# Making u and v as pairs by three products of w_in in place of four, in a fused FNet-mixing and spatial-gating kernel

## The chip, the cores and the metric

The kernel runs on one core of a Trainium2 chip. The metric is the device time of one execution in microseconds (us). Engines are called as the profile calls them: PE multiplies matrices, PEld loads its weights, DVE is the vector engine, ACT the activation engine, POOL the third elementwise engine, SP the engine that here only issues transfers.

## The reference

```python
X = fft(fft(x, axis=1), axis=2).real              # x: 8 x 3072 x 256
h = maximum(X @ w_in, 0)                          # w_in: 256 x 1024
u, v = h[..., :512], h[..., 512:]
v_n = (v - mean(v)) / sqrt(var(v) + 1e-6)         # over the last axis
v_s = einsum('ts,bsd->btd', w_spatial, v_n) + b_spatial[None, :, None]
out = (u * v_s) @ w_out                           # out: 8 x 3072 x 256
```

The largest part by far is the product with `w_spatial` (W below), 3072 x 3072, for each of the 8 batches.

## The kernel before

The transform over time is a sum of a part that is even in the time s and one that is odd. So with E the even part's product with `w_in` and O the odd part's, time s has E + O and time 3072 - s has E - O. The kernel keeps both parts in a tile `eo`, and the weights in `weo`. For time s it multiplies with `weo`, for time S - s with the same first half and the negated second, `wom`: two products for each, four for the two. In batch 0 it also turns W by transposes on PE, piece by piece, and writes it back to memory in the turned form; later batches only load it.

One batch is 24 steps: six chunks of 512 times, each with four groups g of six tiles of v. While PE makes the spatial products of batch b, the preparation of batch b + 1 (folds of x on DVE, the transforms, v) is put into the same steps. The parts that matter here, with cuts:

```python
psM = tile_pool(name="psM", bufs=4, space=PSUM)     # four banks, shared by all but pw
NWR = 6                                             # buffers for loaded pieces of W

def v_tile(b, i, eo, v, pr):                        # one tile of 128 times
    pv = psM.tile([P, DH], FP32, name="pv", tag="psM")
    for kt in range(2):                             # w: weo, or weo and wom for i >= 12
        nc.tensor.matmul(pv, lhsT=l, rhs=w, start=(kt == 0), stop=(kt == 1))
    nc.scalar.activation(out=r, in_=pv, func=AF.Relu)
    nc.vector.bn_stats(out=stt[:, jj, :], in_=r)
    nc.vector.bn_aggr(out=mv[:, jj, :], in_=stt[:, jj, :])
def v_root(pr): ...                                 # ACT: sqrt(var + eps) of two tiles
def v_norm(b, v, pr): ...                           # ACT scales one tile, DVE the other

def s_v(i):                                         # the queue's order, batches 1 to 7
    if i % 2 == 0 and i: v_norm(b, v, pr)           # of the two tiles before
    v_tile(b, i, eo, v, pr)

for dt in range(NDT):                               # one step
    spatial(cur["v"], wts[ti], pws[dt], g, dt)      # six matmuls of 512 columns
    if g == NG - 1: gts.append(gate(c, pws[dt], uts[dt]))
    piece()                                         # batch 0: turn one more piece of W
    ...                                             # project, u_tile, the step's preparation
```

## Time and profile before

1469.43 us is the median of four runs (1468.79 to 1474.39). The profiled execution spans 1471.1 us.

| | before |
|---|---|
| busy share PE / DVE / ACT / POOL | 93% / 50% / 32% / 9% |
| granted clock over the whole kernel | 0.975 |
| start to the first output tile's copy out of PSUM | 153.1 us |
| from there to the same copy of batch 1 | 191.4 us |
| the same from batch to batch, 1 to 6 (mean of 5) | 168.2 us |
| batch 6 to 7; batch 7 to the end | 163.5; 122.0 us |

The copy of a batch's first output tile (`ot`, on ACT, in its fifth step) I call the mark of a batch.

### The profile page before, as it was taken

The numbers are of one execution on the slowest core, as the hardware profiler recorded it, in microseconds if no ns is written. First come the engines' busy times: TensorE is split into PE (matmuls) and PEld (weight loads), VectorE is DVE, ScalarE is ACT, GpSimd is POOL, SyncE is SP. The second block draws the span as 40 slices with busy tenths as digits, with TensorE's granted clock in tenths as the row PEclk, the third lists the DMA queues.
The fourth block names the chain that finished last, engine by engine and source line by source line (L and its number), as shares of the span: only waits on it lengthen the run. The fifth ranks groups of instructions, "written<-read, shape, count | busy, mean of one in ns | idle before, by whom it ended". The sixth has DMA issues, their size and how long they took to land.

```text
span 1471.1 us, 18005 instructions
## 1 busy us (share of the span) xinstructions
PE 1372.1 (93%) x7071; PEld 673.5 (46%) x7071; DVE 740.0 (50%) x1491; ACT 464.2 (32%) x779; POOL 133.7 (9%) x187
## 2 busy tenths in 40 slices
PE   0667999999999999999999999999999999999998
PEld 0333455544444444444444444444444444444444
DVE  6757745555355634655344733565345643561212
ACT  3554235521244123431244113431244212441111
POOL 7622434410000000000000000000000000000000
PEclk9878999999999999999999999999999999999999
DMA  7863999795333543346334463336344443434441
GB/s 258 282 223 125 329 337 297 259 330 180 129 129 126 196 163 124 122 141 224 122 129 133 151 203 129 129 122 228 130 138 141 151 159 122 144 127 157 143 158 50
DMA packets 100597, 255.28 MB, mean 174 GB/s; under 512 B 13568, under 2 KB 60192, under 8 KB 100384
## 3 DMA queue, kind: packets, MB, share of 16 engines
q1 hardware_dynamic: 61440, 196.66, 39.4%
q10 hardware_dynamic: 29568, 44.05, 8.2%
q0 software_dynamic: 9504, 13.42, 2.8%
q8 instruction: 55, 0.90, 0.2%
q14 instruction: 30, 0.25, 0.0%
HBM read 210.80 MB, written 56.62 MB: 182 GB/s over the span
## 4 chain that ended last, share of the span: by engine, by line
PE 84%; DVE 7%; ACT 1%; issue 1%; ACTq 0%; DVEq 0%
PE pw L496 63%; PE po L512 6%; PE pu L488 5%; PE pv L454 5%; DVE tm L501 2%; PE pt L151 1%; PE pe L408 1%; DVE gt L504 1%; DVE sm L308 1%; DVE xt L328 1%; DVE stt L458 1%; DVE of L330 0%; DVE ef L312 0%; ACT v_t L472 0%; ACT r L457 0%
## 5 line engine op out<-in xcount | busy, mean ns | idle before, releaser
L496 PE MATMUL pw<-wt,v_t 128*128 128x512 bf16 x4608 | 1084.5, 382 | 37.6 <-DVE tm L501 23.4
L496 PEld LDWEIGHTS <-v_t 128*128 128x128 bf16 x4608 | 451.6, 98 | 581.2 <-issue 41.3
L501 DVE TENSOR_TENSOR tm<-pw,bbc 128x512 f32<-128x512 f32 x192 | 131.0, 682 | 263.5 <-PE pw L496 263.5
L490 ACT ACTIVATE ut<-pu 128x512 bf16<-128x512 f32 x192 | 114.6, 597 | 318.0 <-PE pu L488 213.2
L458 DVE BATCH_NORM_STATS2 stt<-r 128x6 f32<-128x512 f32 x192 | 132.6, 690 | 162.0 <-ACT r L457 162.0
L516 ACT COPY ot<-po 128x512 f32<-128x512 f32 x96 | 56.3, 586 | 309.6 <-PE po L512 308.0
L504 DVE TENSOR_TENSOR gt<-tm,ut 128x512 bf16<-128x512 f32 x192 | 135.8, 707 | 13.8 <-DVE tm L501 0.5
L457 ACT ACTIVATE r<-pv 128x512 f32<-128x512 f32 x192 | 111.0, 587 | 100.5 <-PE pv L454 91.3
L472 ACT ACTIVATE v_t<-r,rs 128x512 bf16<-128x512 f32 x96 | 78.1, 813 | 105.1 <-DVE rs L470 104.4
L512 PE MATMUL po<-wob,gt 128*128 128x256 bf16 x768 | 103.6, 279 | 1.4 <-DVE gt L504 1.4
L488 PE MATMUL pu<-eo_t,weo 128*128 128x512 bf16 x288 | 95.1, 385 | 2.4 <-ACT r L457 2.4
L454 PE MATMUL pv<-weo,eo_t 128*128 128x512 bf16 x288 | 94.7, 385 | 0.8 <-DVE wt L154 0.3
L512 PEld LDWEIGHTS <-gt 128*128 128x128 bf16 x768 | 76.8, 101 | 32.4 <-issue 3.3
L156 ACT COPY wt<-pt 128x768 bf16<-128x768 bf16 x53 | 42.0, 800 | 61.4 <-PE pt L151 61.0
L469 DVE RECIPROCAL rs<-rs 128x2 f32<-128x2 f32 x96 | 15.5, 162 | 89.0 <-ACT rs L465 89.0
L151 PE MATMUL pt<-ident,wb 128*128 128x128 bf16 x576 | 50.6, 231 | 6.9 <-ACT r L457 2.8
L454 PEld LDWEIGHTS <-eo_t 128*128 128x128 bf16 x384 | 37.2, 100 | 41.8 <-issue 2.7
L151 PEld LDWEIGHTS <-wb 128*128 128x128 bf16 x576 | 42.4, 104 | 29.0 <-issue 7.0
L474 DVE TENSOR_SCALAR v_t<-r,mv,rs 128x512 bf16<-128x512 f32 x96 | 52.7, 549 | 0.0
L146 POOL CAST wb<-wr 128x768 bf16<-128x768 f32 x48 | 42.6, 895 | 78.4 <-PE pt L151 46.9
L143 POOL CAST wb<-wr 128x768 bf16<-128x768 f32 x48 | 42.1, 887 | 70.3 <-PE pt L151 40.2
L410 ACT ACTIVATE eo_t<-pe,spb 128x384 bf16<-128x384 f32 (+1 forms) x32 | 35.8, 1117 | 37.8 <-PE pe L408 37.8
(218 smaller groups left out, 664.2 us busy)
## 6 DMA issues: line engine op xcount, KB each, us to landing
wt<-wtd SPq DMA_DIRECT2D x168, 768.0 KB, 4.4
wr<-in_moe_w_spatial_dram SPq DMA_DIRECT2D x96, 384.0 KB, 5.2
out_dram<-ot ACTq DMA_DIRECT2D x96, 256.0 KB, 3.9
wtd<-wt ACTq DMA_DIRECT2D x24, 768.0 KB, 5.3
xr<-in_x_dram POOLq DMA_DIRECT2D x32, 384.0 KB, 11.7
xt<-in_x_dram SPq DMA_DIRECT2D x21, 512.0 KB, 4.0
xt<-xr SPq DMA_DIRECT2D x21, 512.0 KB, 5.0
x<-in_x_dram SPq DMA_DIRECT2D x1, 1536.0 KB, 6.6
```

What stands on the lines that cost most here:

```text
L151: nc.tensor.transpose(pt[:, kk, :], wb[:, 128 * kk:128 * kk + 128], ident)
L454: nc.tensor.matmul(pv, lhsT=l, rhs=w, start=(kt == 0), stop=(kt == 1))
L457: nc.scalar.activation(out=r, in_=pv, func=AF.Relu)
L458: nc.vector.bn_stats(out=stt[:, jj, :], in_=r)
L472: nc.scalar.activation(out=v[:, i - 1, :], in_=r2[0], func=AF.Identity, scale=rs[:, 0:1], bias=rs[:, 2:3])
L488: nc.tensor.matmul(pu, lhsT=w, rhs=r, start=(kt == 0), stop=(kt == 1))
L490: nc.scalar.activation(out=ut, in_=pu, func=AF.Relu)
L496: nc.tensor.matmul(pw, lhsT=v[:, k, 128 * dt:128 * dt + 128], rhs=wt[:, kk, :], start=(k == 0), stop=(k == KT - 1))
L501: nc.vector.tensor_tensor(out=tm, in0=pw, in1=bbc[:, TC * c:TC * c + TC], op=ALU.add)
L504: nc.vector.tensor_tensor(out=gt, in0=tm, in1=ut, op=ALU.mult)
L512: nc.tensor.matmul(po[:, i, :], lhsT=gts[dt][:, t0:t0 + 128], rhs=wob[:, dt, :], start=(dt == 0), stop=(dt == NDT - 1))
L516: nc.scalar.copy(out=ot, in_=po)
```

## The change

Its intent: PE is full, so take products off it. With P = eo times weo (two products: E + O) and M = 2 O (one product with doubled weights, `wo2`), time s is P, and time S - s is P - M. ACT copies M out of PSUM, and DVE subtracts it from P. u is paired in the same way, so its chunks are reordered (`ORDER`) and the upper ones shifted by one row, which makes the last tile of chunk 3 of 127 rows plus the single row of time S/2. The W pieces pair columns likewise, the first nine are cast by ACT rather than POOL, and the folds of x move to steps without gates.

```diff
-NWR = 6
+NWR = 5
+ORDER = [0, 3, 1, 4, 2, 5]
+def t_base(c):
+    return TC * c if c < 3 else 2561 - TC * (c - 3)
...
+    def w_rows(c, r):
+        t0 = t_base(c) + P * r
+        if c == 3 and r == 3:
+            return [(0, P - 1, t0), (P - 1, 1, S // 2)]
+        return [(0, P, t0)]
...
-            nc.gpsimd.tensor_copy(out=wb, in_=wr)
+            if first:
+                nc.scalar.copy(out=o_, in_=i_)
+            else:
+                nc.gpsimd.tensor_copy(out=o_, in_=i_)
...
+    def v_pair(i, eo, pr):
+        for kt in range(2):
+            nc.tensor.matmul(pv, lhsT=eo[:, kt, sl], rhs=weo[:, kt, DH:], start=(kt == 0), stop=(kt == 1))
+        nc.tensor.matmul(pd, lhsT=eo[:, 1, sl], rhs=wo2[:, DH:], start=True, stop=True)
+        nc.scalar.activation(out=r[0], in_=pv, func=AF.Relu)
+    def v_minus(i, eo, pr, pv, pd):
+        nc.scalar.copy(out=m_, in_=pd)
+        nc.vector.tensor_tensor(out=r[1], in0=pv, in1=m_, op=ALU.subtract)
+        nc.vector.bn_stats(out=stt[:, 0, :], in_=r[0])
+        nc.scalar.activation(out=r[1], in_=r[1], func=AF.Relu)
...
+            if c == 3 and h == 1:       # output: 128 rows, 127 rows, one row
+                nc.scalar.dma_start(out=..., in_=ot[:, 0, :])
+                nc.scalar.dma_start(out=..., in_=ot[0:P - 1, 1, :])
+                nc.scalar.dma_start(out=..., in_=ot[P - 1:P, 1, :])
...
+                    if i:                                   # the queue's order of a pair
+                        st_[s][q].append(lambda i=i: self.vn(i - 1))   # scaling of i - 1
+                    st_[s][q].append(lambda i=i: self.va(i))           # products, first relu
+                    st_[s][q].append(lambda i=i: self.vb(i))           # copy, subtraction, statistics
+                    st_[s][q + 1].append(lambda i=i: self.vr(i))       # root
```

## The prediction

> **What bounds the kernel now.** I read, in order, the busy times of the page, busy time by stretch, the timelines of PE and VectorE (DVE) around one batch start, then the groups of instructions that the change touches.
>
> ```profile
> PE 1372.1 (93%) x7071; PEld 673.5 (46%) x7071; DVE 740.0 (50%) x1491; ACT 464.2 (32%) x779; POOL 133.7 (9%) x187
> ...
> 0.00:81.00 81.00, 27.18 (x170) 14.28 (x171) 57.49 (x89) 35.39 (x48) 53.08 (x90) 0.89 0.82 280
> 81.00:132.00 51.00, 37.25 (x189) 17.70 (x186) 28.11 (x74) 27.09 (x49) 9.78 (x12) 0.80 0.49 172
> 132.00:309.00 177.00, 170.21 (x1120) 93.42 (x1121) 108.15 (x203) 72.16 (x115) 70.83 (x85) 0.98 0.83 293
> 646.00:814.00 168.00, 164.81 (x812) 79.40 (x810) 85.04 (x179) 50.98 (x88) 0.00 (x0) 0.99 0.45 151
> 1319.00:1471.00 152.00, 146.65 (x734) 71.46 (x731) 35.72 (x58) 23.49 (x40) 0.00 (x0) 1.00 0.38 128
> ```
>
> The columns of a stretch are its length, then PE, weight load, DVE, ACT and POOL busy, the granted clock, the DMA share and GB/s. There are three stages. Up to 132 us (tables, folds, first tiles of v) PE has many gaps. From 132 to 309 us batch 0 also turns W, and DMA is 83% busy. Then come batches of 168 us, in which PE lacks only 3.2 us; the last one, with nothing to prepare, takes 152. So PE bounds batches 1 to 7. Its gap, at a batch's fourth step:
>
> ```profile
> 832.65 5.34 PE L496 MATMUL pw<-wt,v_t 128*128 128x512 bf16 x24
> 837.83 0.59 PE L488 MATMUL pu<-eo_t,weo 128*128 128x512 bf16 x2
> 838.26 4.21 PE L496 MATMUL pw<-wt,v_t 128*128 128x512 bf16 x18
> 845.66 2.72 PE L496 MATMUL pw<-wt,v_t 128*128 128x512 bf16 x6 [3.19 <-DVE tm L501]
> ...
> 844.85 0.17 DVE L341 COPY ho<-od 128x2 bf16<-128x2 bf16 x1
> 844.92 0.69 DVE L501 TENSOR_TENSOR tm<-pw,bbc 128x512 f32<-128x512 f32 x1
> ```
>
> The folds of x stand on DVE between the last gates of a chunk; the fourth gate is late, its PSUM bank is not free, and PE waits 3.19 us. The next six matmuls take 2.72 us, while twelve elsewhere in the chain take 2.59: 0.216 us each, or about double after the gap. The gap thus costs 3.2 + 1.4 + some 0.3 in the projection behind it = 4.9 us.
>
> The groups that I use:
>
> ```profile
> L501 DVE TENSOR_TENSOR tm<-pw,bbc 128x512 f32<-128x512 f32 x192 | 131.0, 682 | 263.5 <-PE pw L496 263.5
> L490 ACT ACTIVATE ut<-pu 128x512 bf16<-128x512 f32 x192 | 114.6, 597 | 318.0 <-PE pu L488 213.2
> L458 DVE BATCH_NORM_STATS2 stt<-r 128x6 f32<-128x512 f32 x192 | 132.6, 690 | 162.0 <-ACT r L457 162.0
> L457 ACT ACTIVATE r<-pv 128x512 f32<-128x512 f32 x192 | 111.0, 587 | 100.5 <-PE pv L454 91.3
> ...
> 77.84 0.29 ACT L465 ACTIVATE rs<-mv,epst 128x2 f32<-128x2 f32 x1 [1.75 <-DVE mv L459]
> 78.68 0.81 ACT L472 ACTIVATE v_t<-r,rs 128x512 bf16<-128x512 f32 x1 [0.54 <-DVE rs L470]
> 79.40 0.58 ACT L457 ACTIVATE r<-pv 128x512 f32<-128x512 f32 x1
> ```
>
> The last three give hand-over times: from a square root's start to the scaling of v is 0.84 us, and a following activation starts 0.72 us after that one.
>
> **What the Trainium skill says.** "TensorE: Matmul & The Clock Gate", section "Wait — 56ns, not 53.3ns?", gives 215.7 ns per warm matmul of 512 columns and 426.7 cold: the trace agrees (216, and about 450 after the gap). Its section "Architectural detail" calls the ACT and DVE queues strictly first in, first out: everything below rests on that, and the trace agrees (the late gate behind the folds). "ScalarE: Activation LUTs", section "What ACT_TABLE_LOAD costs", gives 186 ns + 0.833 ns per element, 613 ns for 512; the trace has 587 from PSUM. I take 0.61 us for the new relu from SBUF. "DMA: Bandwidth & Descriptors", section "Why a DMA increments its semaphore by 16 and not by 1", says that a transfer whose outer dimension is 127 runs on one of the 16 engines; the kernel before has no such transfer, so its trace shows nothing of it.
>
> **The change part by part.**
>
> 1. Fewer products. v needs 3 x 12 matmuls of 512 columns per batch in place of 48, u likewise: 24 fewer x 0.216 = 5.2 us per batch, 41.5 us in all, on the bounding engine. Added: the column of time S/2, two matmuls of 512 for v (0.43) and eight of one column for u (about 0.45, an estimate from the 0.055 us pitch of 128-column transposes). Net per batch 4.3.
>
> 2. Folds moved off the gate steps (now steps 0, 1, 4, 5, 8, 9 of a batch): the 4.9 us gap goes in batches 1 to 6, and about 4 us in batch 0.
>
> 3. What is added off PE. Each pair has one more ACT copy out of PSUM (0.59) and one DVE subtraction (0.69, as tm); v's second relu now starts only after the subtraction. In sum DVE gets 24 x 0.69 = 17 us per batch on 85, ACT nothing much for u and 12 x 0.6 for v on 51. Neither engine becomes full.
>
> 4. The serial chain of a v pair. In the new queue order ACT runs scaling of pair i-1, relu, copy, second relu, root of pair i, and only then scaling of i; each step waits for DVE. One turn: 0.72 (scaling to next start) + 0.49 (relu to next start) + 0.59 (copy) + 0.04 + 0.69 (subtract) + 0.04 + 0.61 (relu) + 0.04 + 0.69 (statistics) + 0.04 + 0.18 (aggregate) + 0.04 + 0.84 (root to scaling) = 5.0 us. Nothing of pair i overlaps pair i-1.
> The 12 pairs stand in steps 14 to 23 of a batch. PE's own time there: 40 groups of six spatial matmuls x 1.30 = 52, pairs 12 x 0.65 = 7.8, four u pairs 2.6, four projections 3.5: 66 us. The chain: 12 x 5.0 = 60; in each of the three gate steps (15, 19, 23) gate 0 (1.4) stands before one pair's reciprocal and gates 1 to 3 (4.2) before the next, less 0.4 of overlap: 5.2 x 3 = 15.6; the u pairs' copies and subtractions add about 1 us x 4. Sum about 80, which is 14 more than PE has.
> Can PE run ahead? A pair takes two of the four shared PSUM banks, so it can by about one and a half pairs. I walked the built queues bank by bank with these durations: PE waits about 5 us in steps 16 and 17 (a u product needs the bank that pair 3's copy frees), 5 in steps 20 and 21 (late gates, then pair 8's bank), 2 at the next batch's start (gates behind pair 11). I take 12.2 us per preparation.
>
> 5. Start. ACT casts nine W pieces (two casts of 384 elements, about 1.0 us, on top of a 0.8 us copy), so POOL, which in the kernel before casts while a 1.23 us fold takes 4.95, leaves DVE alone. DVE gains about 12 us up to the end of the folds, but ACT's nine pieces at about 2.5 us each, with the width products, end no earlier. I count zero. The nine pairs in batch 0's first three steps take 9 x 5.4 + 4 = 53 us, as the 51 now.
>
> 6. W in batch 0. The last rows of chunk 3 are loaded as 127 + 1, four times. If 127 rows use one engine: 390 KB at 348 GB/s / 0.96 / 16 = 22.6 GB/s (window 150 to 200 us) is 17 us each, against 5.2 now. They are wanted one step (17 to 20 us) apart, so most hides; I count 10 us.
>
> Sum. Batches 1 to 6: 168.0 - 4.9 - 4.3 + 12.2 = 171.0, +3 x 6 = +18. Batch 7: -2 (u only). Batch 0: -4.3 - 4 + 12.2 + 2 (W evacuations in the chain) + 10 = +16. Total +32: 1502 us.
>
> **Rivals.** (a) The chain hides behind PE. For it: no engine is full, and the present order, with pairs of tiles in twelve steps, never stalls there. Against: the 5.0 us turn and four banks. It would give 1502 - 7 x 12.2 = 1417, with the start in its favour 1405. (b) Batch 0 is bounded by DMA: 83% busy now, pieces of 1.5 KB rows in place of 3, and one engine holding a piece; wasted time could be 40 us, 1530. (c) The start gains the 12 us on DVE: 1490. (d) POOL casts slow the chain's DVE steps in batch 0 as they slow the folds: another 10 us.
>
> **Range and chances.** The chain's surplus is the difference of two sums near 70, so 7 us either way per batch is fair: 7 x 7 = 49 us at the extremes. With batch 0 at plus or minus 15, eight in ten lie in 1448 to 1540. Faster by 2% (under 1440) needs most stalls absent: 0.14. Within 2% (to 1499): 0.38. Slower: 0.48.
>
> **What would show it.** Right: a period near 171 us of which PE is busy 159; PE idle before pud, po and pd products, released by ACT copies and DVE subtractions, in steps 16, 17, 20 and 21; root-to-root time of v pairs 5 us or more; no 3.2 us gap in step 4; W pieces with landing times near 17 us. Wrong: a period near 159 us, with PE full during the pairs (rival a); or PE idle before transposes in 132 to 309 us (rival b).

## More of the kernel before

From the page, the shares of the chain that ended last; and from the groups, the scaling of v on ACT (busy us, mean ns, then idle time before it and what ended it):

```profile
PE 84%; DVE 7%; ACT 1%; issue 1%; ACTq 0%; DVEq 0%
...
L472 ACT ACTIVATE v_t<-r,rs 128x512 bf16<-128x512 f32 x96 | 78.1, 813 | 105.1 <-DVE rs L470 104.4
```

PE carries 84% of the chain. ACT waits 104 us before its scalings, but beside a full PE, so they cost nothing.

## The result

The changed kernel takes 1555.62 us, the median of four runs (1552.24 to 1559.46): slower by a ratio of 1.058 (95% interval 1.0546 to 1.0613). A ratio here is the mean time of one kernel's fast runs over the mean of the other's of the same rounds, so not quite the ratio of the medians quoted. The profiled execution spans 1553.5 us at a granted clock of 0.959. The direction is as predicted; 1555.62 lies outside the range of 1448 to 1540.

The page of the changed kernel: busy times, the shares of the chain that ended last, and two groups.

```profile
PE 1365.8 (88%) x6955; PEld 657.5 (42%) x6955; DVE 854.3 (55%) x1715; ACT 516.7 (33%) x897; POOL 153.0 (10%) x278
...
PE 57%; DVE 18%; ACT 9%; DMA 5%; issue 4%; POOL 3%; ACTq 2%; SPq 1%; DVEq 0%; POOLq 0%
...
L505 ACT ACTIVATE v_t<-r,rs 128x512 bf16<-128x512 f32 x96 | 78.1, 813 | 185.6 <-DVE rs L503 181.6
...
L521 PE MATMUL pud<-eo_t,wo 128*128 128x512 bf16 x96 | 37.2, 387 | 31.2 <-ACT m__8779 L481 3.5
```

PE's share of the chain fell from 84% to 57%, and DVE, ACT and DMA took it over. PE is busy for only 6 us less than before. ACT's wait before its scalings rose from 104 to 182 us, and PE waits 31 us before the third product of u's pairs, which the kernel before does not have.

Cut at the marks (58 and 57 are the first transform's copy out of PSUM), the busy times by stretch, before and then after. The columns are a stretch's limits and length, then PE, weight load, DVE, ACT and POOL busy, the granted clock, DMA share and GB/s:

```profile
57.00:153.00 96.00, 71.30 (x389) 35.55 (x388) 59.28 (x130) 44.67 (x72) 25.16 (x30) 0.80 0.58 203
153.00:344.00 191.00, 185.12 (x1169) 98.99 (x1168) 114.27 (x222) 73.36 (x118) 63.95 (x78) 0.99 0.85 297
344.00:1186.00 842.00, 826.03 (x4057) 397.59 (x4055) 426.38 (x892) 255.33 (x441) 0.00 (x0) 0.99 0.45 151
...
1349.00:1471.00 122.00, 116.65 (x583) 56.69 (x580) 26.33 (x40) 18.38 (x31) 0.00 (x0) 1.00 0.36 123
```

```profile
58.00:180.00 122.00, 72.21 (x389) 34.10 (x388) 60.59 (x136) 53.23 (x88) 33.46 (x66) 0.74 0.47 153
180.00:386.00 206.00, 186.80 (x1157) 98.16 (x1155) 127.94 (x251) 79.43 (x131) 82.05 (x147) 0.97 0.81 275
386.00:1261.00 875.00, 817.29 (x3985) 386.77 (x3983) 504.63 (x1031) 282.66 (x506) 0.00 (x0) 0.98 0.43 145
...
1434.00:1553.00 119.00, 113.90 (x572) 55.56 (x569) 33.20 (x48) 15.62 (x28) 0.00 (x0) 1.00 0.38 126
```

| stretch | before | after | difference |
|---|---|---|---|
| start to the first transform | 57.4 | 58.3 | +0.9 |
| first transform to batch 0's mark | 95.8 | 122.1 | +26.3 |
| batch 0's mark to batch 1's | 191.4 | 205.9 | +14.5 |
| batch 1's to batch 6's mark, five periods | 841.1 | 874.5 | +33.4 (6.7 each) |
| batch 6's to batch 7's mark | 163.5 | 173.6 | +10.1 |
| batch 7's mark to the end | 122.0 | 119.1 | -2.9 |

The differences sum to 82.4 us, the difference of the spans. In the five steady periods PE was busy 817 in place of 826 us, so products were saved, but it was idle 58 in place of 16 us: a new wait took more than the saving.

That wait, in the timeline of one pair of v (start, length, then in brackets the idle time before it and its releaser):

```profile
818.92 0.81 ACT L505 ACTIVATE v_t<-r,rs 128x512 bf16<-128x512 f32 x1 [4.43 <-DVE rs L503]
...
820.12 0.57 ACT L481 COPY m__7276<-pd 128x512 f32<-128x512 f32 x1
820.73 0.69 DVE L482 TENSOR_TENSOR r<-pv,m__7276 128x512 f32<-128x512 f32 x1 [1.45 <-ACT m__7276 L481]
820.74 1.03 PE L557 MATMUL po<-wob,gt 128*128 128x256 bf16 x8 [1.04 <-ACT m__7276 L481]
...
823.06 0.30 ACT L497 ACTIVATE rs<-mv,epst 128x2 f32<-128x2 f32 x1 [0.98 <-DVE mv L493]
...
823.90 0.81 ACT L505 ACTIVATE v_t<-r,rs 128x512 bf16<-128x512 f32 x1 [0.54 <-DVE rs L503]
...
825.72 0.59 PE L521 MATMUL pud<-eo_t,wo 128*128 128x512 bf16 x1 [3.52 <-ACT m__7312 L481]
...
826.10 2.77 PE L541 MATMUL pw<-wt,v_t 128*128 128x512 bf16 x6
```

From one scaling to the next is 4.98 us; the prediction's walk had 5.0. ACT's copy of the next pair stands behind the root and scaling of this one, which wait for DVE. The copy's PSUM bank therefore comes free late, and PE, which wants it for u's third product, waits 3.52 us. The next six matmuls take 2.77 us, where six take 1.46 elsewhere in the same view: PE is cold after the gap. In this preparation PE waits 1.04 and 3.52 us in step 16, 0.89, 1.04 and 2.22 in step 20 and at its end, and 0.94 at the next batch's start, about 10 us. The 0.89 and the 0.94 are waits for gates on DVE, the other four for ACT's copies.

The Trainium skill, "TensorE: Matmul & The Clock Gate", section "What's actually happening", says that the clock goes down after at least one idle window of about 3.4 us, and that this window runs freely. The trace agrees only in part: the granted clock falls from 1.00 to 0.50 at 824.35 us, only 2.15 us into the gap, and in the 3.41 us before that PE was busy for 1.27 us (by the profile's modelled ends of matmuls). So the window was not idle throughout.

Batch 0 has two things more. First, the loads of W. In the view of the transfers between 60 and 170 us, the row of what they moved, in 40 slices:

```profile
GB/s 324 284 351 91 203 273 110 24 43 322 304 233 118 147 24 75 241 25 46 337 86 24 23 24 23 25 216 225 22 252 65 25 24 26 123 324 23 149 302 64
```

For slices on end it moves 22 to 26 GB/s. Those are the pieces of 127 rows; with the rows cut otherwise (below) the runs of such slices are gone. The issue of a W load, and the ACT engine beside it, in two views of the changed kernel, one of the source line of the loads and one of the timeline:

```profile
L148 SPq DMA_DIRECT2D wr<-in_moe_w_spatial_dram x100: 272/368/18654, 1.8 to 308.6; - x100
```

```profile
140.15 0.33 ACTq L184 DMA_DIRECT2D wtd<-wt  x1
140.52 0.60 ACT L524 ACTIVATE up<-pu 128x512 bf16<-128x512 f32 x1 [13.74 <-DMA wr<-in_moe_w_spatial_dram]
...
143.80 0.61 PE L541 MATMUL pw<-wt,v_t 128*128 128x512 bf16 x1 [18.85 <-ACT v_t L505]
```

The three numbers of the first are the shortest, median and longest time of an issue in ns: one takes 18.65 us, where the loads of the kernel before all take under 0.8. The four long ones, 15.4 to 18.65 us, are the single rows, each issued behind a piece of 127 rows. In the second, ACT stands for 13.74 us in front of the store of turned W until a W load has landed, and behind it PE waits 18.85 us for v. Without these events the steps are still long, as the experiments show.

Second, the last row of chunk 3's output is stored behind 127 rows. Per batch, from the timeline of ACT:

```profile
769.12 3.67 ACTq L568 DMA_DIRECT2D out_dram<-ot  x1
772.84 0.60 ACT L524 ACTIVATE up<-pu 128x512 bf16<-128x512 f32 x1 [4.48 <-issue]
```

The issue of the single row takes 3.67 us here (1.68 to 6.98 in the eight batches), behind the store of 127 rows, and ACT does nothing meanwhile.

### The profile page after: what moved, and what is told of

It is laid out like the page before. It is cut to its first block, busy times and chain, and to the rows that moved or that the text cites. A ratio compares the mean times of both kernels' runs of the same rounds, so it can differ in the third digit from the quotient of the medians.

```text
span 1553.5 us, 18360 instructions
## 1 busy us (share of the span) xinstructions
PE 1365.8 (88%) x6955; PEld 657.5 (42%) x6955; DVE 854.3 (55%) x1715; ACT 516.7 (33%) x897; POOL 153.0 (10%) x278
## 4 chain that ended last, share of the span: by engine, by line
PE 57%; DVE 18%; ACT 9%; DMA 5%; issue 4%; POOL 3%; ACTq 2%; SPq 1%; DVEq 0%; POOLq 0%
PE pw L541 44%; DMA wr<-in_moe_w_spatial_dram 5%; PE po L557 4%; DVE tm L547 4%; DVE gt L548 4%; DVE r L482 3%; ACT r L474 2%; DVE stt L483 2%; DVE stt L492 2%; PE pu L519 2%; PE pt L176 1%; ACTq L568 1%; PE pe L432 1%; ACT v_t L505 1%; SPq L148 1%
## 5 line engine op out<-in xcount | busy, mean ns | idle before, releaser
L170 POOL CAST wb<-wr 128x384 bf16<-128x384 f32 (+1 forms) x174 | 97.5, 591 | 178.3 <-issue 59.5
L176 PE MATMUL pt<-ident,wb 128*128 128x128 bf16 x576 | 55.4, 235 | 56.8 <-ACT wb L168 43.1
L524 ACT ACTIVATE up<-pu 128x512 bf16<-128x512 f32 x96 | 57.6, 600 | 117.8 <-PE pu L519 49.5
L484 ACT ACTIVATE r<-r 128x512 f32<-128x512 f32 x96 | 60.5, 630 | 72.8 <-DVE r L482 72.8
L548 DVE SCALAR_TENSOR_TENSOR gt<-up,tm 128x512 bf16<-128x512 bf16 x96 | 67.4, 702 | 3.3
L548 DVE SCALAR_TENSOR_TENSOR gt<-um,tm 128x512 bf16<-128x512 bf16 x96 | 66.7, 695 | 3.3
L470 PE MATMUL pv<-weo,eo_t 128*128 128x512 bf16 x192 | 60.7, 398 | 7.5 <-ACT wt L181 3.2
L521 PE MATMUL pud<-eo_t,wo 128*128 128x512 bf16 x96 | 37.2, 387 | 31.2 <-ACT m__8779 L481 3.5
L474 ACT ACTIVATE r<-pv 128x512 f32<-128x512 f32 x96 | 55.6, 579 | 19.6 <-PE pv L470 19.6
L519 PE MATMUL pu<-eo_t,weo 128*128 128x512 bf16 x192 | 57.1, 379 | 1.0 <-DVE wt L179 1.0
```

Of the source, the lines that this page charges most:

```text
L170: nc.gpsimd.tensor_copy(out=o_, in_=i_)
L176: nc.tensor.transpose(pt[:, kk, :], wb[:, 128 * kk:128 * kk + 128], ident)
L470: nc.tensor.matmul(pv, lhsT=eo[:, kt, sl], rhs=weo[:, kt, DH:], start=(kt == 0), stop=(kt == 1))
L474: nc.scalar.activation(out=r[0], in_=pv, func=AF.Relu)
L519: nc.tensor.matmul(ps, lhsT=weo[:, kt, wd], rhs=eo[:, kt, sl], start=(kt == 0), stop=(kt == 1))
L548: nc.vector.scalar_tensor_tensor(out=gt, in0=ut, scalar=0.0, in1=tm, op0=ALU.max, op1=ALU.mult)
```

## The experiments

All gave a correct result. Each time is the median of four runs, in three rounds; the kernel before took 1469.83 us in the first group, 1471.05 in the second, 1471.46 in the third and 1471.92 in the fourth. All are edits of the changed kernel; the diffs show the main lines alone.

My theory after reading the result: (1) the pair's chain costs PE some 12 us per preparation because a bank is freed late; (2) the transfers of 127 rows hold up loads in batch 0 and ACT in each batch; (3) the start on ACT costs nothing. The rivals: the third product's DVE and ACT work as such is too much; or batch 0 is bound by the amount that DMA moves.

**Rows of the W loads cut so that no transfer has 127 rows.** The rows go as 112 + 15 + 1.

```diff
-            return [(0, P - 1, t0), (P - 1, 1, S // 2)]
+            return [(0, 112, t0), (112, 15, t0 + 112), (P - 1, 1, S // 2)]
```

> The changed kernel, but the last rows of chunk 3 of W are loaded as 112 + 15 + 1 rows in place of 127 + 1; nothing else is touched. Theory (one DMA engine carries a 127-row load, and the loads behind it cannot even be issued): the four loads no longer hold up the first steps of batch 0, the stretch from the first spatial product to the end of the v pairs of batch 0 falls from 84 us to some 55, and the time falls by 30 to 40 us, to 1515 to 1525. Rival (the long landing times are the price of 1.5 KB rows in place of 3 KB, or of a DMA that is full anyway): less than 8 us.

1548.09 us (1538.45 to 1554.46), ratio 1.052 [1.0468, 1.0572]. Only 8 us: a miss. That is the number of the rival, but not its cause: the long issues and the runs of slices at 22 to 26 GB/s do go. The stretch from the first spatial product to the last scaling of batch 0's v on ACT falls from 87.9 only to 74.6 us (51.5 in the kernel before). The longest issue of a load falls from 18.65 to 1.23 us and batch 0's mark from 180.4 to 167.6, still far from 153.1. Something else holds these steps at nearly the same length; and a part of the 12.8 us is given back later (the steady period of this trace is 175.9).

**Rows of the output store cut likewise.**

```diff
-    nc.scalar.dma_start(out=..., in_=ot[0:P - 1, 1, :])
+    for p0, n in ((0, 112), (112, 15)):
+        nc.scalar.dma_start(out=..., in_=ot[p0:p0 + n, 1, :])
```

> The changed kernel, but the output of chunk 3 is stored as 112 + 15 + 1 rows in place of 127 + 1. Theory (the issue of the one-row store stands on ACT's queue for 1.7 to 7 us [...], and ACT's evacuations behind it hold PSUM banks): the issue falls below 0.5 us, PE's two gaps of 0.8 and 0.6 us in step 9 of each batch go, batch 0 gains up to 7 us, in all 8 to 15 us, to 1541 to 1547. Rival (the gap is covered by other waits): under 3 us.

1544.46 us (1538.9 to 1546.78), ratio 1.0496 [1.047, 1.0521]: 11 us, as expected, and all of it in the steady batches, where the period goes from 174.9 to 172.6 and the two gaps of step 9 are gone. Batch 0 gains nothing (205.9 us to the next mark in both), where up to 7 us were expected: there the issue is short, but ACT now stands in front of it, 7.42 us in all in place of 8.05.

**v by four products again, u still by three.**

```diff
-    nc.tensor.matmul(pd, lhsT=eo[:, 1, sl], rhs=wo2[:, DH:], start=True, stop=True)
+    nc.tensor.matmul(pd, lhsT=eo[:, 0, sl], rhs=weo[:, 0, DH:], start=True, stop=False)
+    nc.tensor.matmul(pd, lhsT=eo[:, 1, sl], rhs=wo2[:, DH:], start=False, stop=True)
...                        # wo2: negated for v; relu of pd, no copy and subtraction
```

> The changed kernel with v alone back to four products: the minus half comes from two matmuls with signed weights, so the copy of pd and the subtraction go; u stays paired. Theory (the serial chain of a v pair, 5.0 us a turn, is what stalls PE): the turn falls to about 3.8 us, the stalls of 10 to 13 us per batch mostly go, at a price of 12 x 0.216 = 2.6 us of PE per batch; period from 174 to about 165 to 167, time down by 50 to 60 us to 1495 to 1505. Rival (PE's work bounds, the stalls only move): period 174 or more, time 1555 to 1575.

1495.4 us (1493.29 to 1495.55), ratio 1.0164 [1.0149, 1.018]: 60 us less, as expected. So v's pairs carry most of the loss. But this batch 0 has its mark at 179.2 us, as late as with v's pairs. With the rows cut as well (below) it is at 154.8: the 127-row loads alone keep it there.

**The same three products, the root and scaling later.** In batches 1 to 7 a pair's root and scaling stand behind the next pair's products, copy and statistics. The instructions stay the same; `r` gets a fourth buffer, which was not tried alone.

```diff
-                    if i:
-                        st_[s][q].append(lambda i=i: self.vn(i - 1))
                     st_[s][q].append(lambda i=i: self.va(i))
                     st_[s][q].append(lambda i=i: self.vb(i))
-                    st_[s][q + 1].append(lambda i=i: self.vr(i))
+                    if i:
+                        st_[s][q + 1].append(lambda i=i: self.vr(i - 1))
+                        st_[s][q + 1].append(lambda i=i: self.vn(i - 1))
```

> The changed kernel with the same arithmetic and the same products, but in batches 1 to 7 the root and the scaling of a v pair stand in the queues behind the next pair's relu, copy and subtraction (one more buffer pair for r), so that two pairs overlap. Theory (order in the queues, not the amount of work, makes the chain): the turn falls to about 3.5 to 4 us, PE's gaps in the pair steps fall from 10 to under 3 us per batch, the period from 174 to about 163, time down by 55 to 75 us to 1480 to 1500. Rival (DVE and ACT do too much work there, or four PSUM banks are too few in any order): less than 25 us gained.

1487.93 us (1487.73 to 1488.35), ratio 1.0117 [1.0102, 1.0132]: 68 us less, with as many instructions on every engine (1715 on DVE, 897 on ACT in both). That decides for the order of the queue against the amount of work as the cause, and against four banks being too few in any order. By the trace the fourth buffer alone would not help: in the steady batches of the changed kernel no relu and no subtraction of v waits for a buffer of `r` (they wait for PE, for ACT's copy or for the subtraction). The turn itself, expected at 3.5 to 4 us, is 5.6 on average.

**Both cuts of rows together.**

> The changed kernel with both row fixes (W loads and output stores of chunk 3 as 112 + 15 + 1). The two alone gave about 8 and 11 us. If they act in different places (the loads up to 165 us, the stores once per batch), the sum holds: 1533 to 1540. If both only moved the same slack, 1543 to 1548.

1530.89 us (1530.09 to 1531.66), ratio 1.0407 [1.0391, 1.0422]: 25 us less than the changed kernel, more than the two alone (8 + 11). The steady period is 172.3. From here on all versions but one have both cuts.

**Both cuts and the late root.**

> Both row fixes and the later root and scaling in batches 1 to 7; products as in the changed kernel. Sum of the parts measured: 1488 - 19 = 1469, period near 163 us against 168 before. So it should stand within 1462 to 1476, level with the kernel before: what is gained in the steady batches is lost in the first 230 us.

1461.42 us (1460.75 to 1462.52), ratio 0.9935 [0.992, 0.995], just under the expected range. Its steady period is 162.7. One such period of it, and one of the version with only the rows cut:

```profile
688.90:851.80 162.90, 159.89 (x798) 76.69 (x797) 99.85 (x207) 56.13 (x102) 0.00 (x0) 1.00 0.46 155
```

```profile
720.70:892.50 171.80, 161.83 (x798) 76.92 (x797) 100.71 (x207) 56.68 (x102) 0.00 (x0) 0.99 0.44 147
```

PE makes the same 798 products. Its idle time falls from 10.0 to 3.0 us and its busy time by 1.9, at a clock of 1.00 in place of 0.99. DVE and ACT do the same work in both.

**Both cuts, and no pairing at all.** As the edit above for v, and u likewise.

> Both row fixes, and neither u nor v by three products: all of the change but the pairing of products. Theory: u's pairing is worth its 12 x 0.216 = 2.6 us of PE per batch, since its copy and subtraction stand on no chain: about 1475 (rows and v alone) + 8 x 2.2 = 1493, 1485 to 1500. Rival: u's extra copy and subtraction cost as much as they save: 1470 to 1480. In both, slower than the kernel before although it does nearly the same products, which puts some 20 us or more on the first 230 us (W layout, loads, queue order).

1467.11 us (1466.74 to 1467.57), ratio 0.9973 [0.9958, 0.9988]. A miss for both expectations, 1485 to 1500 and 1470 to 1480. The rest of the change (order of chunks, moved folds, W by column pairs) thus costs nothing in sum once the rows are cut. Its mark of batch 0 is at 150.3 us, the next 193.8 later.

**POOL casts the first nine pieces, as before the change.**

```diff
-            if first:
-                nc.scalar.copy(out=o_, in_=i_)
-            else:
-                nc.gpsimd.tensor_copy(out=o_, in_=i_)
+            nc.gpsimd.tensor_copy(out=o_, in_=i_)
```

> The changed kernel with the first nine W pieces cast on POOL again. Up to the end of the ninth piece ACT is now the longest (57 us; the folds end at 45). Theory: POOL casts beside ACT's copies, the pieces end earlier, the folds slower: net -6 to +2 us. Rival (the casts on ACT are what they were meant to be, a gain, since POOL casts slow the folds by up to 4 times): +5 to +12 us.

1547.99 us (1545.78 to 1551.39), ratio 1.0531 [1.0513, 1.0548]: 8 us less, slightly beyond the theory's range. The first transform is at 53.9 us in place of 58.3, and batch 0's mark comes 4.6 us earlier. The rest of the 8 us lies in later batches, which the edit does not touch. The casts on ACT were no gain: they freed DVE, which finished the folds at 44.7 us and then waited 12.52 us for PE's products of the sums behind ACT's pieces.

**Both cuts, v by four and u by three.**

> The changed kernel with the 127-row transfers cut (112 + 15 + 1) and v back to four products, while u stays paired by three. Against the version with no pairing at all (1467.1) only u's pairing differs. Theory (the copy and the subtraction of u's pairs give back the PE time they save): the 60 us of v and the 25 us of the rows add up, 1555 - 85 = 1470, so 1465 to 1474. Rival (u's pairing earns its PE time, about 2 us a batch once the rows no longer disturb): 1448 to 1458.

1457.92 us (1456.56 to 1458.69), ratio 0.9913 [0.9897, 0.9929]. The theory had 1465 to 1474: a miss, the rival was right. u's three products shorten the steady period from 166.6 to 164.0, and lengthen batch 0 up to its second mark by 7.4 us (351.5 against 344.1). It is 37 us faster than the same without the cuts, where the changed kernel gained 25.

**Both cuts, late root, POOL casts.**

> Rows cut, root and scaling of a pair after the next pair's work in batches 1 to 7 (together 1461.4), and the casts of the first nine W pieces back on POOL (alone -8 from the changed kernel). Theory (the start is a part of its own, so its gain adds): 1451 to 1456. Rival (batch 0's later chain of pairs and W swallows it): 1459 to 1463.

1457.16 us (1456.56 to 1460.64), ratio 0.9914 [0.9895, 0.9933]: 4 us below the version without POOL's casts, between the two expectations. The first transform is 4.5 us earlier (53.9 against 58.4), batch 0's mark 3.9 (163.3 against 167.2).

**The late root in batch 0 too.** The last pair of each step still has its root and scaling at the end of the step.

```diff
-                    steps[s_][q].append(lambda i=i: me.vr(i))
-                    steps[s_][q + 1].append(lambda i=i: me.vn(i))
+                    for k in ([i - 1] if q else []) + ([i] if q == 2 else []):
+                        e = steps[s_][q + (k == i)]
+                        e.append(lambda k=k: me.vr(k))
+                        e.append(lambda k=k: me.vn(k))
```

> As the run with rows, late root and POOL casts, and in batch 0 too a pair's root and scaling stand behind the next pair's products, subtraction and statistics (at the end of a step for its last pair). Theory (batch 0's first three steps are long because the pairs run one after another with PE waiting for their end and they for PE): these three steps fall from about 75 us to 55 to 65, so 10 to 20 us less than that run: 1432 to 1444. Rival (what counts there is that the step's last pair must end before PE goes on, and the pieces of W in between): within 4 us of it, 1449 to 1457.

1452.74 us (1451.59 to 1453.49), ratio 0.9878 [0.9862, 0.9894]: 4.4 us less, where the theory had 10 to 20: the rival was nearer. From the first spatial product to the last scaling of batch 0's v it is 68.1 us in place of 74.5. Batch 0's mark comes 6.4 us earlier, and half of that is lost by the next. PE still waits 1.8 to 3.9 us at a time for v, two or three times a step.

**Four products in batch 0 only.** In batches 1 to 7 all stays paired. A second set of negated weights, `wo1`, is made by DVE out of PSUM.

```diff
+        if four: nc.tensor.matmul(pd, lhsT=eo[:, 0, sl], rhs=weo[:, 0, DH:], start=True, stop=False)
-        nc.tensor.matmul(pd, lhsT=eo[:, 1, sl], rhs=wo2[:, DH:], start=True, stop=True)
+        nc.tensor.matmul(pd, lhsT=eo[:, 1, sl], rhs=(wo1 if four else wo2)[:, DH:], start=not four, stop=True)
...                        # u likewise; four = (b == 0)
+                    nc.vector.tensor_scalar(out=wo1[...], in0=pw_, scalar1=sgn[:, 0:1], op0=ALU.mult)
```

> As the run with rows, late root and POOL casts, but batch 0 makes u and v by four products as the kernel before does; batches 1 to 7 by three. Theory (the pairs' three products cost batch 0 the 15 to 20 us by which its period differs between the versions with and without pairing, 160.5 and 141.7 less some 4 that any batch differs): 1433 to 1441, which beats the kernel before by 2%. Rival (that time was hidden under W's loads afterwards): 1447 to 1456.

1441.81 us (1440.85 to 1444.79), ratio 0.9808 [0.9785, 0.983]: 15 us less, just above the theory's range; whether it is 2% faster than the kernel before is unclear by the interval. My own edit put the first transform 7 us later (61.3 in place of 53.9). The timeline of DVE shows the reading of the width products ahead of the folds:

```profile
35.45 0.75 DVE L326 TENSOR_SCALAR wo<-pw__320,sgn 128x512 bf16<-128x512 f32 x1 [11.12 <-ACT wo L324]
```

**The negated weights by POOL, after the folds.**

```diff
-                    nc.vector.tensor_scalar(out=wo1[...], in0=pw_, scalar1=sgn[:, 0:1], op0=ALU.mult)
+    nc.gpsimd.tensor_scalar(out=wo1, in0=weo[:, 1], scalar1=sgn[:, 0:1], scalar2=None, op0=ALU.mult)
     specials_out(*sp_)
```

> As the version with four products in batch 0 (1441.8), but the negated sine weights that they need are made by POOL from the finished table after the folds' casts, not by DVE from PSUM ahead of the folds. Theory (DVE's wait of 11.12 us there delayed the start by 7 us): first marker back from 61.3 to 54 to 55 us and 5 to 8 us less: 1434 to 1437. Rival (the start is hidden under W's loads that follow): 1440 to 1444.

1436.62 us (1434.17 to 1439.85), ratio 0.9766 [0.9741, 0.979]. The first transform is at 55.1 us again, and the time is 5 us less: as the theory expected. So three products in batch 0 cost 20.5 us in all (1457.16 - 1436.62).

**And the late root in batch 0.**

> The same, with a pair's root and scaling behind the next pair's work in batch 0 too (4.4 us with three products). Theory (both shorten the same wait of PE for the last pair of a step, so they add only in part): 0 to 4 us less than the run before it, 1431 to 1437. Rival (with two evacuations in place of three and a subtraction the chain is short enough, and the added delay of the earlier pairs costs): 1 to 4 us more.

1433.79 us (1432.42 to 1436.8), ratio 0.9746 [0.9721, 0.9771]: 3 us less, within the theory's range; but the times of the two versions overlap, so the difference is not shown by them. In the traces batch 1's mark is 4.4 us earlier (338.7 against 343.1). This is the fastest version found: 2.5% faster than the kernel before, and 122 us faster than the change as it was given.

## Why the prediction was right or wrong

**Step 1, fewer products, and step 2, the fold gap: right.** The prediction had 168.0 - 4.9 - 4.3 = 158.8 us of PE's own time per period. With rows cut and the late root PE is busy 159.89, and the 3.2 us gap of step 4 is gone.

**Step 4, the chain of a pair: right in mechanism and place; the close size is partly luck.** Predicted was a 5.0 us turn, and waits of 5 us in steps 16 and 17, 5 in 20 and 21 and 2 at the next batch's start. Measured is a turn of 4.98, and waits of 4.6, 4.2 and 0.9 us, about 10 in sum. Some 2 us of cold clock, which the walk did not name, make up most of the rest: with the rows cut the period is 172.3, which is 12.4 above 159.9. The late root takes 9.6 of them away (172.3 to 162.7) without taking away an instruction. A bare turn does not become short by it (775.06 to 780.26 us is one scaling to the next there, 5.2 us), but the turns around the gates do (from 8.87 to 5.8 us and less), and the eleven turns of a preparation take 62.2 in place of 74.9 us. What helps, as I read the queues, is that the copy that frees a bank no longer stands behind the root and scaling of the pair just before it, only behind those of the pair before that.

**The steady period, 171.0 predicted, 174.9 measured: a part was missing.** With the output's rows cut it is 172.6. The prediction named 127-row loads of W only; that the output of chunk 3 is stored in 127 rows too, in every batch, is nowhere in its sum. Cutting it is worth 2.3 us a period (11 us in all). Of these the trace shows 1.4 us as waits of PE behind ACT (0.77 and 0.64 us in step 9); where the rest falls I did not pin down.

**Step 5, "The nine pairs in batch 0's first three steps take 9 x 5.4 + 4 = 53 us, as the 51 now": this step failed.** From the first spatial product to the last scaling of batch 0's v on ACT the kernel before takes 51.5 us and the changed one 87.9. With the rows cut, which takes step 6's loads away, it is still 74.5. So this step grew by 23 us where the prediction had 2. With no pairing it is 62.0, so the pairs account for 12.5 of them; the other 10.5 I did not take apart. From the first transform to batch 0's mark the change took 26.3 us longer. With the rows cut it is still 12.7 longer, and 16.4 longer than with no pairing (108.5 against 92.1 us). 5.4 us was little more than the bare turn of 5.0. In batch 0 the turn has more on it, as the version with cut rows shows in a step (ACT, PE, then ACT twice):

```profile
105.36 0.81 ACT L505 ACTIVATE v_t<-r,rs 128x512 bf16<-128x512 f32 x1 [1.34 <-DVE rs L503]
...
106.23 1.89 PE L541 MATMUL pw<-wt,v_t 128*128 128x512 bf16 x4 [5.26 <-ACT v_t L505]
...
109.65 0.60 ACT L474 ACTIVATE r<-pv 128x512 f32<-128x512 f32 x1 [3.48 <-PE pv L470]
...
113.30 0.78 ACT L181 COPY wt<-pt 128x768 bf16<-128x768 bf16 x1
...
114.46 0.59 ACT L526 COPY m__968<-pud 128x512 f32<-128x512 f32 x1
...
116.39 0.81 ACT L505 ACTIVATE v_t<-r,rs 128x512 bf16<-128x512 f32 x1 [1.34 <-DVE rs L503]
```

PE waits for the step's last pair (5.26 us), then works cold; meanwhile ACT waits 3.48 us for PE's next pair, as its products stand behind PE's spatial products of the new step. The two wait for each other in turn, once a step. Between a pair's root and its scaling stand a copy of turned W and the relu and copy of a u pair, whose subtraction stands before the reciprocal on DVE. So this turn took 11.0 us in place of 5.4, the one before it 7.9, and only the bare one 5.0. The kernel before pays 3.30 us for the same wait in a step:

```profile
100.58 1.04 PE L496 MATMUL pw<-wt,v_t 128*128 128x512 bf16 x2 [3.30 <-ACT v_t L472]
```

The prediction added a copy of W here and there but not the u pairs, of which batch 0's first chunk has four, and not the answer time of PE. Against rival (b), it is no shortage of DMA: from the first transform to batch 0's mark DMA is 47% busy. Of (b), one engine holding a piece is real; that is step 6. Its sign, PE idle before transposes from 132 us to batch 1's mark, is there too (10.1 us in place of 1.2), but 6.1 of it is the wait behind the one-row store told below. Rival (d) is out: in batch 0 the subtraction takes 0.69 us and the statistics 0.68 and 0.66, as in the later batches.

**Step 6, the W loads, 10 us predicted: right in size, incomplete in mechanism.** Cutting them gave 12.8 us at batch 0's mark (13.6 with the output's rows cut too), but only 8 us in the end when the stores stayed. The prediction had a load of about 17 us that mostly hides. What it did not have is that the issue of the next transfer blocks (18.65 us), so that later pieces, not only this one, come late, and that ACT's store stands behind such a load. The loads and the pairs overlap: either alone keeps batch 0's mark at 167 to 180 us, and with both gone it is at 150 to 155. So each experiment alone undervalued its cause, and rows were worth 37 us with v by four products but 25 with pairs.

**Batch 0's second part, about +6 predicted, +14.5 measured.** The chain of batch 1's pairs is worth 12.5 us there too (209.1 to 196.6 by the late root). But the 8.3 us by which step 1 and 2 were to shorten it do not show: 196.6 is above the 191.4 of the kernel before. With four products in batch 0 and the late root it is 190.4. A part of it is one wait. With both cuts and the late root PE is idle 12.4 us there, in place of 5.9, and 5.6 of it are these (ACT, then PE's transposes of W):

```profile
217.98 0.60 ACT L524 ACTIVATE up<-pu 128x512 bf16<-128x512 f32 x1 [7.25 <-DMA out_dram<-ot]
...
219.10 0.80 PE L176 MATMUL pt<-ident,wb 128*128 128x128 bf16 x6 [5.60 <-ACT m__1997 L526]
```

ACT stands 7.25 us at the stores of chunk 3's output, and the copy behind them frees the bank that PE wants. So in batch 0 cutting the output's rows did not remove that wait. Why it stays there I did not test; DMA is 84% busy in this stretch.

**Step 5, the start, counted zero against rival (c): right, +0.9 us.** The gain on DVE was real (folds done at 44.7 in place of 60.2 us) and went into a wait behind ACT, as argued. POOL's casts show that zero was not the best to be had: 4 us.

**Step 3 and batch 7: right.** No engine became full (DVE 55%, ACT 33%); batch 7 gave -2.9 for -2.

In sum, by the spans, the change cost 82.4 us and the prediction had 32. Of the 50 us between, 26 lie in the start and batch 0 (41.8 against 16), and 26 in the six periods from batch 1's mark to batch 7's (43.5 against 18); batch 7 gives 1 back. A steady period is 3.7 us above the predicted growth: 2.3 for the stores of 127 rows, and 1.4 by which the terms for the chain and for PE's own work were too low together. The sixth period (+10.1 against +3) holds the first steps of batch 7, where the kernel before had no gap to be taken away (163.5 in place of 168.2).

## What to carry to other kernels

Work taken from the bounding engine is worth its time only if the hand-overs that replace it do not hold that engine's buffers: put whatever frees a buffer ahead of whatever only finishes a result, in each engine's queue. Where a stage has its own limit, as batch 0 has here, count the chain with everything that stands in the queues of that stage, and choose the form for each stage by itself: four products in batch 0 and three in the others beat both. When two causes hold the same stretch, take both away before judging either.

## What the Trainium skill lacked or had wrong

- "DMA: Bandwidth & Descriptors", section "Why a DMA increments its semaphore by 16 and not by 1": that 127 rows run on one engine agrees (22 to 26 GB/s in the trace, where one sixteenth of the full rate was put at 22.6). It doesn't say what it does to the issuer: the one-row transfer issued behind it took up to 18.65 us of SP's queue and 1.68 to 6.98 of ACT's, and an engine that computes is idle for it. Cutting the rows into 112 + 15 + 1 brought the longest issue of a load to 1.23 us; for the stores it freed ACT in the steady batches, but in batch 0 ACT still stood 7.42 us at them.
- The same page, section "Issuing engines are not separate DMA queues": it says that the time to initiate a transfer is usually small relative to the transfer. The median of 0.37 us agrees; the 18.65 us is the case in which it doesn't hold.
- "TensorE: Matmul & The Clock Gate", section "What's actually happening": an idle window of about 3.4 us before the clock goes down. In these traces the window need not be idle throughout. In the kernel before the granted clock falls at 845.52 us, in a gap of 3.19 us, with PE busy for 0.35 us of the 3.41 before; in the changed kernel it falls at 824.35 us with PE busy for 1.27 us of the 3.41 before. I cut four traces (the kernel before, the changed one, the cut rows without and with the late root) from 100 us on into windows of 3.41 us that end where the clock falls. A fall followed windows with up to 1.65 us of busy PE, and every window at full clock with less than 1.43 us was followed by one. PE's busy time goes by the profile's modelled ends of matmuls.
